# Windowed attention feeding a mixture of experts: searches for the largest w2, scaled w2 operands made in steps, and two row blocks of the last products interleaved

## The chip, the cores and the metric

The kernel runs on one core of a Trainium2 chip. The time is in device microseconds (us), the median of a few executions. The engines are called PE (TensorE, the matmuls), ACT (ScalarE), DVE (VectorE), POOL (GpSimd) and SP (SyncE, which issues all the transfers here).

## The reference

An attention with a window and block summaries, whose output is the input of four experts, mixed with given weights. Cut to what matters:

```python
def _attn_ref(q, k, v):                       # (4, 8, 768, 64), block 32, window 16
    k_sum = k.reshape(B, H, nb, block, D).max(axis=3)
    v_sum = v.reshape(B, H, nb, block, D).mean(axis=3)
    scores_l = where(abs(pos_i - pos_j) < window, scale * q @ k.T, -1e9)
    scores_s = scale * q @ k_sum.T + np.log(block)
    a = softmax(concatenate([scores_l, scores_s], -1))
    return a @ concatenate([v, v_sum], 2)

def _moe_ref(x, domain_probs, w1, w2):        # x 3072 x 512, 4 experts, hidden 1024
    p = domain_probs / (domain_probs.sum(-1, keepdims=True) + 1e-09)
    out = 0
    for e in range(4):
        h = np.maximum(x @ w1[e], 0.0)        # first products
        out += p[:, e:e + 1] * (h @ w2[e])    # second products
    return out
```

All inputs and the output are f32.

## The kernel before, in words

The 3072 tokens are eight blocks of 384 (`TB`). The attention works in 64 pieces; each gives scores (tile `psc` in PSUM), their exponentials (`ms`, with the negated maximum `nb`), a transpose over DRAM (`aw`, `awT`) and the values (`px`), and writes rows of x to DRAM, from where they are read as operands of the experts. f32 numbers are split into a high and a low half, and each product is three matmuls: high by high, high by low, low by high (`hh` and `hl` are the halves of the hidden activations, `xh` and `xl` those of x).

The program is written as a plan of stages (L1191). Three plain stages treat blocks 0 to 1; then the pairs of blocks 1, 2 and 3 follow (`PAIRS`, L807): pair 1 goes through the experts 3, 2, 1, 0, pair 2 through 0, 1, 2, 3, and pair 3 through 3, 2, 1, 0. Each pair and expert is one stage (`pair_units`, L1074). A stage has first products, x by w1, for four groups i of two hidden blocks (f1, f2), in a form with seven products instead of eight (`SEVEN`, L993). Its tiles are `pha` to `phd`: after product 0 ACT copies `pha` into a new `phb`, after product 1 ACT copies `phd` into an SBUF tile `p5`, after product 2 DVE adds it to `phb` to make `phc`, and so on; the later products add onto these. Then the stage has second products, h by w2.

In pairs 1 and 2 the second products are plain (`po` tiles, 128x512). In pair 3, called `SCALED` (L151), they too have the form with seven products (`second_seven`, L1039), in f16 and for three row blocks t of 128 rows in each of the two token blocks. Product m has 12 matmuls of 128x256; the tiles are `poa` to `pod`, named with the expert and t, so that `pob2_1` is tile b of expert 2 and t = 1. After product 0 ACT copies `poa` into `pob`, after product 1 ACT copies `pod` into `p6`; product 2 adds onto `pob`. The copies run under a raised priority (`RUSH`).

To use f16 there, h, w2 and v are scaled by powers of two, which need the largest magnitude of w1 and of w2 for each expert, and of v. `scan` (L751) is called 16 times for an expert, for eight blocks of w1 and eight of w2, each a DVE reduction into a column of `found`. It is called in the stages of pair 1: for w1 in `w1_operands` (L774), for w2 in `pair_units` after products 4 and 5 (L1137). The sixteenth call reduces the columns, and `over_partitions` (L123) takes the maximum over the 128 partitions: 128x2 numbers go to DRAM (`w3d` for expert 3), a second transfer reads them back broadcast to all partitions (`w3e`), DVE reduces that, and `scales` (L131) makes the powers of two. For v the tiles are `vd` and `ve`.

`make_w2` (L811) makes pair 3's scaled w2 operands while pair 2 is computed. There are 16 groups (e, i). One call loads the two raw blocks of a group (`wr2s`, tag `wr` with four buffers), makes four parts and writes each to DRAM (`ws`): a part `wp` is ACT's scaled f16 copy, then DVE's f16 remainder, then a transfer on SP. Between parts POOL makes the differences of the raw blocks in place. Parts 0 and 1 take buffers of tag `wr`, which the raw loads of w1 and w2 use also; parts 2 and 3 take the tag `chunk`, or `ms` once pair 3's x operands exist, with two buffers each. `wp0_23` is part 3 of expert 0's group 2. Calls come after the last first product of group number 1 in pair 2's stages e = 1 to 3 (L1140), and at the unit numbers in `MAKE` (L998) in the second products (`with_fetch`, L946). The stage of pair 3 reads the parts back (`w2s`).

From a point early on (`pinned["rest"] = False`) the order on each engine isn't the written one: a scheduler in the compiler orders the instructions by a timeline of its own, with the written order and the raised priorities as its input. Every engine's instruction goes through one helper line, so all have line 79 in the profile, and the tiles tell them apart.

Of the kernel before, what the change touches and what calls it, by code (L numbers as in the profile page):

```python
# [17 lines left out]
P = 128  # L18
# [48 lines left out]
def attn_moe(ctx: ExitStack, tc: tile.TileContext, qvL, qv0, v0L, kD, kT, vT, w1L, w2L, dpL, cst, out):  # L67
# [54 lines left out]

    def over_partitions(m, k, name):  # L123
        room = dram.tile([P, k], F32, name=f"{name}d")
        SP.dma_start(room, m)
        every = sb.tile([P, P, k], F32, name=f"{name}e", tag="hs", bufs=2)
        flat = room.rearrange("p k -> (p k)").rearrange("(o n) -> o n", o=1)
        SP.dma_start(every.rearrange("p q k -> p (q k)"), flat.broadcast_to([P, P * k]))
        V.tensor_reduce(m, every.rearrange("p q k -> p k q"), axis=AX.X, op=ALU.max)

# [71 lines left out]
    def setup_v(b):  # L202
        vsr = sb.tile([P, G, NB], F32, name=f"vsr{b}", tag="vsr")
        top = facts(G) if b == SCALED else None
        for hp in range(H // 2):
            ch = chunk(f"vch{b}_{hp}")
            load_chunk(b, hp, ch, vT)
            block_stats(ch, vsr, hp, ALU.add)
            if b == SCALED:
                V.tensor_reduce(  # L210
                    top[:, hp : hp + 1], ch, axis=AX.X, op=ALU.max, apply_absolute_value=True
                )
        stack_v(b, vsr)
        if b == SCALED:
            m = facts(1)
            V.tensor_reduce(m, top, axis=AX.X, op=ALU.max)
            over_partitions(m, 1, "v")
            v_scale[b] = scales(m, 1, "v")

# [531 lines left out]
    def scan(e, which, fc, part):  # L751
# [12 lines left out]
        if len(seen) == 2 * FC:  # L764
            m = tops["m"]
            V.tensor_reduce(m, t, axis=AX.X, op=ALU.max)
            over_partitions(m, 2, f"w{e}")
            w_scale[e] = s, inv = scales(m, 2, f"w{e}")
            V.tensor_scalar_mul(s[:, 1:2], s[:, 1:2], W2TOP)
            V.tensor_scalar_mul(inv[:, 1:2], inv[:, 1:2], 1.0 / W2TOP)  # L770

    WS = ("11", "s2", "s1", "s3", "12", "s4", "22")

    def w1_operands(e, pr):  # L774
# [8 lines left out]
        stored[e, pr] = {}  # L783
        scan(e, 0, 2 * pr, r1)
        scan(e, 0, 2 * pr + 1, r2)

# [7 lines left out]
        parts("11", a11, PL)  # L794
        parts("22", a22, V)
        PL.tensor_tensor(a22, a21, a22, op=ALU.add)
        PL.tensor_tensor(a21, a11, a21, op=ALU.subtract)
# [10 lines left out]
    made = {}  # L808
    to_make = [(e, i) for e in PAIRS[-1][1] for i in range(FC // 2)]

    def make_w2():  # L811

        if not to_make:
            return
        e, i = to_make.pop(0)
        s = w_scale[e][0][:, 1:2]
        r1, r2 = (load_weights(w2L, e, 2 * i + j, "2s") for j in range(2))
        r11, r12 = r1[:, 0:256], r1[:, 256:512]
        r21, r22 = r2[:, 0:256], r2[:, 256:512]
        keep = made[e, i] = [dram.tile([P, n, 512], F16, name=f"ws{e}_{i}{n}") for n in (4, 3)]  # L820

        def parts(k, n, raw):
            tag, bufs = ("wr", 4) if k < 2 else ("ms", 2) if SCALED in xpair else ("chunk", CHUNKS)
            t = sb.tile([P, 2, n], F16, name=f"wp{e}_{i}{k}", tag=tag, bufs=bufs)
            A.activation(t[:, 0], raw, AF.Copy, scale=s)
            V.scalar_tensor_tensor(t[:, 1], raw, s, t[:, 0], op0=ALU.mult, op1=ALU.subtract)
            room = keep[k // 2][:, 2 * (k % 2) : 2 * (k % 2) + 2] if k < 3 else keep[1][:, 2]
            SP.dma_start(room if k < 3 else room.rearrange("p (v f) -> p v f", v=2), t)

        parts(3, 256, r11)  # L830
        parts(0, 512, r2)
        PL.tensor_tensor(r11, r12, r11, op=ALU.subtract)
        PL.tensor_tensor(r12, r22, r12, op=ALU.subtract)
        parts(1, 512, r1)
        PL.tensor_tensor(r22, r22, r11, op=ALU.subtract)
        PL.tensor_tensor(r21, r21, r22, op=ALU.subtract)
        parts(2, 512, r2)

# [106 lines left out]

    def with_fetch(units, jobs=()):  # L946
# [92 lines left out]
    def second_seven(pr, e, order, hs, w2):  # L1039
        for t in range(TB // P):  # L1040
            bank = {}

            def new(k):
                room, tag = dict(a=(ps_sc, "sc"), d=(ps_av, "av")).get(k, (ps_mm, "mm"))
                bank[k] = room.tile([P, 512], F32, name=f"po{k}{e}_{t}", tag=tag)[:, 0 : DM // 2]
                return bank[k]

            for m, (k, a, b) in enumerate(SEVEN):
                o = new(k) if m < 2 else bank[k]
                todo = []  # L1050
                for i in order:
                    ah, al = (x[:, t * P : (t + 1) * P] for x in hs[a, i])
                    bh, bl = w2[i][b]
                    todo += [(ah, bh), (ah, bl), (al, bh)]
                for j, (l, r) in enumerate(todo):
                    PE.matmul(
                        o, l, r, start=j == 0 and m < 2, stop=j == len(todo) - 1, skip_group_check=m >= 2
                    )
                with tc.high_priority(offset=RUSH):
                    if m == 0:  # L1060
                        A.copy(new("b"), o)
                    elif m == 1:
                        five = sb.tile([P, TB], F32, name=f"p6{e}_{t}", tag="hs", bufs=2)[:, 0 : DM // 2]
                        A.copy(five, o)
                    elif m == 2:
                        V.tensor_tensor(new("c"), o, five, op=ALU.add)
                    elif m == 4:
                        V.tensor_tensor(bank["d"], o, five, op=ALU.add)
                if m >= 3:
                    k = "adcb"[m - 3]  # L1070
                    add_up((2 * pr + (k in "bd")) * (TB // P) + t, e, bank[k], (k in "cd") * DM // 2)
                yield 2 * len(todo) * US2 / 4, 1.0

    def pair_units(pr, e, last=False):  # L1074
# [11 lines left out]
        for n, i in enumerate(order):  # L1086
# [11 lines left out]
            for m, (k, w, x) in enumerate(SEVEN):  # L1098
# [47 lines left out]
        else:  # L1146
            units = second(tbs, e, hT, w2, last)
        yield from with_fetch(units, MAKE.get((pr, e), ()))

# [132 lines left out]
```

## Time and profile before

| | |
|---|---|
| median of 3 runs | 1194.36 us (1193.41 to 1196.8) |
| the profiled execution | 1199.33 us |
| its span in the trace | 1197.6 us |
| mean granted PE clock | 0.984 |
| PE busy | 1142.4 us, 95% of the span |
| DVE, ACT, POOL busy | 790.8, 634.9, 527.0 us |
| DMA | 275.52 MB, mean 230 GB/s |

By the places of the tiles in the trace, the stages of pair 1 lie at 377 to 446 (e = 3), 446 to 519, 519 to 590 and 590 to 673 us (e = 0); those of pair 2 at 673 to 746 (e = 0), 746 to 815, 815 to 884 and 884 to 953 (e = 3); those of pair 3 at 953 to 1012 (e = 3), 1012 to 1070, 1070 to 1129 and 1129 to 1197 (e = 0).

How to read it: a row of a timeline gives start, duration, engine, line, operation, output tile and input tiles, shapes and types, how many instructions were merged (x), and in brackets the idle time of the engine just before and what ended it. A row of waits gives the tile waited for, its engine or DMA, then total us, times, and the longest.

### The profile page before, as it was taken

How to read it: one execution, taken by the hardware profiler on the slowest of the kernel's cores; microseconds unless marked ns; L12 is line 12 of the kernel's file. 1: busy time of each engine (PE TensorE's matmuls, PEld its weight loads, DVE VectorE, ACT ScalarE, POOL GpSimd, SP SyncE). 2: the span in 40 equal slices, each digit the busy share in tenths (PEclk: the TensorE clock that was granted, in tenths of full speed). 3: DMA queues.
4: the chain of work that ended last, by engine and by line, in shares of the span. 5: the costliest groups of instructions: out<-in, count | busy, mean ns of one | idle time of the engine just before them, and what ended most of it. 6: DMA issues, size and time to landing. Idle time of an engine off the chain costs nothing.

```text
span 1197.6 us, 22374 instructions
## 1 busy us (share of the span) xinstructions
PE 1142.4 (95%) x7620; PEld 1013.5 (85%) x7620; DVE 790.8 (66%) x1834; ACT 634.9 (53%) x1754; POOL 527.0 (44%) x642
## 2 busy tenths in 40 slices
PE   9899899999979999999879899999999999999998
PEld 7788789998968988888778798988888888989896
DVE  6669775657896857668587775765447464646464
ACT  5578667655665636455255564645336261626261
POOL 2398777745876737546246555352115200000000
PEclk9999999999989999999979999999999999999999
DMA  6699797948995888789974799989586771919151
GB/s 235 212 284 303 236 256 229 286 111 249 311 247 147 272 249 231 231 246 305 232 241 111 237 321 287 377 256 344 155 247 223 249 241 29 332 47 323 50 206 54
DMA packets 218753, 275.52 MB, mean 230 GB/s; under 512 B 85136, under 2 KB 123664, under 8 KB 218640
## 3 DMA queue, kind: packets, MB, share of 16 engines
q1 hardware_dynamic: 218640, 274.10, 74.0%
q8 instruction: 60, 0.98, 0.3%
q14 instruction: 53, 0.43, 0.1%
HBM read 185.30 MB, written 71.83 MB: 215 GB/s over the span
## 4 chain that ended last, share of the span: by engine, by line
PE 40%; DMA 4%; DVE 3%; ACT 2%; issue 1%; POOL 1%; SPq 0%; POOLq 0%; ACTq 0%; DVEq 0%
PE po L79 12%; PE phb L79 8%; PE pha L79 5%; PE pob L79 4%; PE phc L79 3%; PE phd L79 2%; PE poa L79 2%; DMA w<-wd 1%; PE poc L79 1%; DMA wr2s<-in_w2L 1%; PE px L79 1%; PE pod L79 1%; PE psc L79 1%; DVE hl L79 1%; POOL wr2s L79 1%
## 5 line engine op out<-in xcount | busy, mean ns | idle before, releaser
L79 PE MATMUL po<-w,hh 128*128 128x512 f32 x1152 | 364.3, 397 | 1.7 <-DVE hl L79 1.7
L79 PEld LDWEIGHTS po<-w,hh 128*128 128x128 f32 x1152 | 213.8, 190 | 47.7 <-DVE hl L79 2.0
L79 PE MATMUL po<-w,hl 128*128 128x512 f32 x576 | 228.1, 398 | 0.0
L79 POOL TENSOR_TENSOR ks<-kr,ks 128x304 fp32r<-128x304 f32 x112 | 99.3, 893 | 124.3 <-ACT ks L79 108.5
L79 ACT ACTIVATE ms<-ms,nb 96x152 f32<-96x152 f32 x256 | 104.3, 415 | 49.9 <-DVE nb L79 49.3
L79 PEld LDWEIGHTS po<-w,hl 128*128 128x128 f32 x576 | 108.8, 189 | 23.8
L79 PE MATMUL phb<-xh_t,w1s 128*128 128x384 f32 x384 | 117.5, 347 | 7.6 <-DVE phc L79 4.4
L79 PE MATMUL pha<-xh,w 128*128 128x384 f32 x384 | 112.2, 338 | 1.9 <-DVE nb L79 1.9
L79 DVE CUSTOM_DVE_ANT_0 ms<-psc,c_sb 96x152 f32<-96x152 f32 x256 | 69.1, 305 | 44.2 <-PE psc L79 41.5
L79 PE MATMUL ph<-xh,wh 128*128 128x384 f32 x256 | 88.1, 348 | 6.0 <-ACT wh L79 4.8
L79 PE MATMUL ph<-xl,wh 128*128 128x384 f32 x256 | 87.5, 342 | 2.4 <-DVE xl L79 2.4
L79 DVE TENSOR_TENSOR aw<-ms,aw 96x512 f16<-96x512 f32 x112 | 77.1, 721 | 18.5 <-ACT aw L79 17.3
L79 ACT CAST aw<-ms 96x512 f16<-96x512 f32 x112 | 53.3, 523 | 66.7 <-issue 42.4
L79 PE MATMUL ph<-xh,wl 128*128 128x384 f32 x256 | 87.3, 342 | 0.3 <-POOL wl L79 0.3
L79 POOL TENSOR_TENSOR wl<-wr,wh 128x512 fp32r<-128x512 f32 x44 | 62.0, 1414 | 44.6 <-ACT wh L79 44.4
L79 PEld LDWEIGHTS phb<-xh_t,w1s 128*128 128x128 f32 x384 | 71.9, 191 | 10.5 <-DVE phc L79 5.2
L79 DVE SCALAR_TENSOR_TENSOR wp<-wr2s,found,wp 128x512 f16<-128x512 f32 (+1 forms) x64 | 50.8, 795 | 45.2 <-ACT wp L79 40.0
L79 ACT CAST ks<-kr 128x304 fp32r<-128x304 f32 x112 | 48.1, 444 | 49.0 <-PE psc L79 31.5
L79 PEld LDWEIGHTS pha<-xh,w 128*128 128x128 f32 x384 | 70.9, 188 | 2.5 <-DVE nb L79 2.2
L79 ACT ACTIVATE wp<-wr2s,found 128x512 f16<-128x512 f32 (+1 forms) x64 | 42.5, 667 | 53.1 <-DMA wr2s<-in_w2L 19.9
L79 PEld LDWEIGHTS psc<-ks,qs 128*96 128x96 f32 x448 | 53.3, 165 | 18.1 <-DVE nb L79 9.8
L79 PE MATMUL psc<-ks,qs 128*96 128x152 f32 x448 | 57.0, 251 | 10.5 <-DVE nb L79 9.5
(209 smaller groups left out, 2794.2 us busy)
## 6 DMA issues: line engine op xcount, KB each, us to landing
w<-wd SPq DMA_DIRECT2D x56, 512.0 KB, 5.5
w1s<-wds SPq DMA_DIRECT2D x112, 256.0 KB, 5.1
w<-wd SPq DMA_DIRECT2D x84, 256.0 KB, 5.1
wr<-in_w1L SPq DMA_DIRECT2D x76, 256.0 KB, 4.3
qv<-in_qvL SPq DMA_DIRECT2D x56, 320.0 KB, 4.4
wd<-w SPq DMA_DIRECT2D x32, 512.0 KB, 4.3
wds<-w1s SPq DMA_DIRECT2D x64, 256.0 KB, 2.8
kr<-in_kD SPq DMA_DIRECT2D x56, 256.0 KB, 4.1
```

Source lines behind the costliest of these rows:

```text
L79: ins = getattr(self.engine, name)(*a, **kw)
```

## The change

Three things are changed.

First, the searches. The calls of `scan` for w2 go from pair 1's first products to its second products, one for each of the units 1 to 8. `over_partitions` becomes two steps: `spread_maxima`, which issues both transfers at unit 10, and `take_maxima`, which reduces and makes the scales at unit 14. v's largest value goes the same way. The calls of `scan` for w1 go behind the first two parts in `w1_operands`.

Second, `make_w2` becomes a generator of 65 steps: the first loads the raw blocks of group 0, and each further step makes one part; the step with a group's first part loads the raws of the next group ahead of it. All four parts take the two buffers of `chunk` or `ms`; none takes `wr`. `MAKE` gives steps in place of groups: every second unit of the second products in pair 2's stages e = 0 to 2 and in pair 3's e = 3 and 2, and every unit in pair 3's e = 1. In pair 2's stages e = 1 and 2 there is a step after each of the four groups of first products.

Third, `second_seven` is written with two row blocks interleaved. Products 0 and 1 of t = 0 and t = 1 come first without the last hidden group, then with it; then products 2 to 6 alternate between the two blocks; t = 2 follows alone.

The diff, cut:

```diff
+    def spread_maxima():
+        for t in pending:
+            m, k, name = t["m"], t["k"], t["name"]
+            room = dram.tile([P, k], F32, name=f"{name}d")
+            SP.dma_start(room, m)
+            t["every"] = every = sb.tile([P, P, k], F32, name=f"{name}e", tag="hs", bufs=2)
...
+            SP.dma_start(every.rearrange("p q k -> p (q k)"), flat.broadcast_to([P, P * k]))
+
+    def take_maxima():
+        while pending and "every" in pending[0]:
+            t = pending.pop(0)
+            V.tensor_reduce(t["m"], t["every"].rearrange("p q k -> p k q"), axis=AX.X, op=ALU.max)
+            t["then"](*scales(t["m"], t["k"], t["name"]))
...
-            over_partitions(m, 2, f"w{e}")
-            w_scale[e] = s, inv = scales(m, 2, f"w{e}")
...
+            pending.append(dict(m=m, k=2, name=f"w{e}", then=then))
...
     def make_w2():
...
+        load(*groups[0])
+        yield
+        for (e, i), after in zip(groups, groups[1:] + [None]):
...
             def parts(k, n, raw):
-            tag, bufs = ("wr", 4) if k < 2 else ("ms", 2) if SCALED in xpair else ("chunk", CHUNKS)
+                tag, bufs = ("ms", 2) if SCALED in xpair else ("chunk", CHUNKS)
...
+            if after:
+                load(*after)
+            parts(3, 256, r11)
+            yield
+            parts(0, 512, r2)
+            PL.tensor_tensor(r11, r12, r11, op=ALU.subtract)
+            PL.tensor_tensor(r12, r22, r12, op=ALU.subtract)
+            yield
...
     def with_fetch(units, jobs=(), e=None, w2=None):
...
+            if w2 and 1 <= n <= FC:
+                scan(e, 1, n - 1, w2[n - 1][0].bitcast(F32))
+            if n == FC + 2:
+                spread_maxima()
+            if n == FC + 6:
+                take_maxima()
             if n in jobs:
-                make_w2()
+                next(making, None)
...
-    MAKE = {(2, 0): (4, 12), (2, 1): (2, 7, 13), (2, 2): (2, 7, 13), (3, 3): (2, 8, 14), (3, 2): (3, 11)}
+    MAKE = {(2, e): range(1, 17, 2) for e in range(3)} | {(3, e): range(1, 21, 2) for e in (3, 2)}
+    MAKE[3, 1] = range(1, 21)
...
     def second_seven(pr, e, order, hs, w2):
-        for t in range(TB // P):
...
+        for js in (range(FC // 2 - 1), range(FC // 2 - 1, FC // 2)):
+            for t in range(2):
+                for m in range(2):
+                    us = product(t, m, js)
+                    if FC // 2 - 1 in js:
+                        after(t, m)
+                    yield us, 1.0
+        for ts, ms in (((0, 1), range(2, len(SEVEN))), ((2,), range(len(SEVEN)))):
+            for m in ms:
+                for t in ts:
+                    us = product(t, m)
+                    after(t, m)
+                    yield us, 1.0
...
-                if m in (4, 5) and pr == PAIRS[0][0]:
-                    fc = (f1, f2)[m - 4]
-                    scan(e, 1, fc, w2[fc][0].bitcast(F32))
-                if m == 6 and n == 1 and pr == SCALED - 1 and e > 0:
-                    make_w2()
+                if m == 6 and pr == SCALED - 1 and e in (1, 2):
+                    next(making, None)
```

What the compiler's scheduler makes of it is seen in the order of the instructions. ACT before, at the start of the second products of pair 3, e = 2; `hh2_3`, `h122_3`, `hs32_3` and `hs42_3` are halves of the last group's hidden activations:

```order
L79 CAST hh2_311_13453<-hr2_3_13437 128x768
L79 COPY pob2_0_13501<-poa2_0_13488 128x256
L79 CAST hh2_3s2_13467<-hr2_3_13437 128x768
L79 CAST h122_3_13481<-hq2_3_13439 128x384
L79 CAST hs32_3_13471<-hk2_3_13438 128x384
L79 COPY p62_0_13516<-pod2_0_13503 128x256
L79 COPY p62_1_13653<-pod2_1_13640 128x256
L79 COPY pob2_1_13638<-poa2_1_13625 128x256
L79 CAST hs42_3_13485<-hq2_3_13439 128x384
```

ACT now, at the same place:

```order
L79 CAST hh2_311_13363<-hr2_3_13347 128x768
L79 COPY pob2_0_13467<-poa2_0_13398 128x256
L79 COPY pob2_1_13481<-poa2_1_13438 128x256
L79 CAST hh2_3s2_13377<-hr2_3_13347 128x768
L79 CAST h122_3_13391<-hq2_3_13349 128x384
L79 CAST hs32_3_13381<-hk2_3_13348 128x384
L79 CAST hs42_3_13395<-hq2_3_13349 128x384
L79 COPY p62_0_13472<-pod2_0_13408 128x256
L79 COPY p62_1_13486<-pod2_1_13448 128x256
```

The copy of block 1's `poa` has moved from behind the two `p6` copies to right behind block 0's. On PE the first two products of blocks 0 and 1 alternate in both orders, up to the first product on `pob`.

ACT before, at the start of pair 3's first stage (e = 3): the first copy `phb3_3_2` of its first group comes right behind the last casts of pair 3's x (`xh3`):

```order
L79 CAST xh3_t2_12067<-xr3_3_12254 128x2x96
L79 CAST xh3_t4_12071<-xr3_3_12254 128x2x96
L79 COPY phb3_3_2_12397<-pha3_3_2_12390 128x384
L79 COPY p53_3_2_12406<-phd3_3_2_12399 128x384
L79 COPY p53_3_3_12489<-phd3_3_3_12482 128x384
L79 COPY phb3_3_3_12480<-pha3_3_3_12473 128x384
```

ACT now, at the same place:

```order
L79 CAST xh3_t4_11993<-xr3_3_12176 128x2x96
L79 ACTIVATE wp0_10_14212<-wr2s0_3_13640,found_74 128x512
L79 ACTIVATE wp0_11_14223<-wr2s0_2_13638,found_74 128x512
L79 ACTIVATE wp0_12_14234<-wr2s0_3_13640,found_74 128x512
L79 ACTIVATE wp0_23_14249<-wr2s0_4_14194,found_74 128x256
L79 ACTIVATE wp0_20_14258<-wr2s0_5_14196,found_74 128x512
L79 ACTIVATE wp0_21_14292<-wr2s0_4_14194,found_74 128x512
L79 COPY phb3_3_2_12319<-pha3_3_2_12312 128x384
L79 COPY p53_3_2_12328<-phd3_3_2_12321 128x384
L79 ACTIVATE wp0_22_14312<-wr2s0_5_14196,found_74 128x512
L79 COPY p53_3_3_12411<-phd3_3_3_12404 128x384
L79 COPY phb3_3_3_12402<-pha3_3_3_12395 128x384
```

Six parts of w2's scaled operands now stand ahead of the first copy, one stands among the copies, and four more follow behind them; before, all 64 parts came ahead of this place. By the order, the first 31 parts now stand between instructions that ran at 658 to 767 us before, none between those at 767 and 885, and 33 from there to those at 970.

SP before, near the end of pair 1's first stage (e = 3), where expert 3's largest values go through DRAM; `w3d` stood 37 rows further up:

```order
L79 DMA wd222_0_5816<-w1222_0_5803 128x512
L79 DMA w3e_5749<-w3d_5747 128x256
L79 DMA wds12_0_5827<-w1s12_0_5799 128x512
L79 DMA wds22_0_5823<-w1s22_0_5798 128x512
L79 DMA wd122_0_5835<-w1122_0_5801 128x512
L79 DMA wds32_0_5831<-w1s32_0_5800 128x512
L79 DMA wr12_4_6289<-in_w1L 128x512
L79 DMA wds42_0_5840<-w1s42_0_5802 128x512
L79 DMA wr12_5_6291<-in_w1L 128x512
```

SP now, at the same place:

```order
L79 DMA wds12_0_5806<-w1s12_0_5778 128x512
L79 DMA wds22_0_5802<-w1s22_0_5777 128x512
L79 DMA wd122_0_5814<-w1122_0_5780 128x512
L79 DMA wds32_0_5810<-w1s32_0_5779 128x512
L79 DMA w3d_6085<-found_74 128x2
L79 DMA wr12_4_6287<-in_w1L 128x512
L79 DMA wds42_0_5819<-w1s42_0_5781 128x512
L79 DMA w3e_6087<-w3d_6085 128x256
L79 DMA wd112_1_6007<-w1112_1_5994 128x512
```

`w3d` and `w3e` are now two transfers apart, at a later place. On DVE the reductions of w2's blocks stand where they stood; the reduction of `w3e` comes later. The places of `vd`, `ve`, `w0d` and `w0e` on SP are unchanged.

More of the change, by code (lines that the diff above doesn't have):

```diff
@@ L216, in setup_v @@
             V.tensor_reduce(m, top, axis=AX.X, op=ALU.max)
-            over_partitions(m, 1, "v")
-            v_scale[b] = scales(m, 1, "v")
+            pending.append(dict(m=m, k=1, name="v", then=lambda *s: v_scale.update({b: s})))
     def stack_v(b, vsr):
@@ L795, in w1_operands @@
         parts("22", a22, V)
+        scan(e, 0, 2 * pr, r1)
+        scan(e, 0, 2 * pr + 1, r2)
         PL.tensor_tensor(a22, a21, a22, op=ALU.add)
@@ L808, in attn_moe @@
     made = {}
-    to_make = [(e, i) for e in PAIRS[-1][1] for i in range(FC // 2)]
     def make_w2():
[L813 to L822, printed above, removed]
-            tag, bufs = ("wr", 4) if k < 2 else ("ms", 2) if SCALED in xpair else ("chunk", CHUNKS)
[L824 to L837, printed above, removed]
@@ new lines, in make_w2, with load, parts @@
+        groups = [(e, i) for e in PAIRS[-1][1] for i in range(FC // 2)]
+        raws = {}
+        def load(e, i):
+            raws[e, i] = [load_weights(w2L, e, 2 * i + j, "2s") for j in range(2)]
+        load(*groups[0])
+        yield
+        for (e, i), after in zip(groups, groups[1:] + [None]):
+            s = w_scale[e][0][:, 1:2]
+            r1, r2 = raws.pop((e, i))
+            r11, r12 = r1[:, 0:256], r1[:, 256:512]
+            r21, r22 = r2[:, 0:256], r2[:, 256:512]
+            keep = [dram.tile([P, n, 512], F16, name=f"ws{e}_{i}{n}") for n in (4, 3)]
+            def parts(k, n, raw):
+                tag, bufs = ("ms", 2) if SCALED in xpair else ("chunk", CHUNKS)
+                t = sb.tile([P, 2, n], F16, name=f"wp{e}_{i}{k}", tag=tag, bufs=bufs)
+                A.activation(t[:, 0], raw, AF.Copy, scale=s)
+                V.scalar_tensor_tensor(t[:, 1], raw, s, t[:, 0], op0=ALU.mult, op1=ALU.subtract)
+                room = keep[k // 2][:, 2 * (k % 2) : 2 * (k % 2) + 2] if k < 3 else keep[1][:, 2]
+                SP.dma_start(room if k < 3 else room.rearrange("p (v f) -> p v f", v=2), t)
+            if after:
[6 more added lines that the diff above has]
+            yield
+            parts(1, 512, r1)
+            PL.tensor_tensor(r22, r22, r11, op=ALU.subtract)
+            PL.tensor_tensor(r21, r21, r22, op=ALU.subtract)
+            yield
+            parts(2, 512, r2)
+            made[e, i] = keep
+            yield
@@ L839, in w2_operands @@
+    making = make_w2()
     def w2_operands(e, i):
@@ L944, in second, with with_fetch @@
             yield from mm2(tb, e, range(TB // P), hT, w2)
-    def with_fetch(units, jobs=()):
+    def with_fetch(units, jobs=(), e=None, w2=None):
         for n, us in enumerate(units):
@@ L1039, in second_seven @@
     def second_seven(pr, e, order, hs, w2):
-        for t in range(TB // P):
[L1041 to L1055, printed above, removed]
+        banks = [{} for t in range(TB // P)]
@@ new lines, in new, with product @@
+        def new(t, k):
+            room, tag = dict(a=(ps_sc, "sc"), d=(ps_av, "av")).get(k, (ps_mm, "mm"))
+            banks[t][k] = room.tile([P, 512], F32, name=f"po{k}{e}_{t}", tag=tag)[:, 0 : DM // 2]
+            return banks[t][k]
+        def product(t, m, js=range(FC // 2)):
+            k, a, b = SEVEN[m]
+            o = new(t, k) if m < 2 and 0 in js else banks[t][k]
+            for j in js:
+                ah, al = (x[:, t * P : (t + 1) * P] for x in hs[a, order[j]])
+                bh, bl = w2[order[j]][b]
+                for v, (l, r) in enumerate(((ah, bh), (ah, bl), (al, bh))):
@@ L1056, in second_seven @@
                     PE.matmul(
-                        o, l, r, start=j == 0 and m < 2, stop=j == len(todo) - 1, skip_group_check=m >= 2
-                    )
[L1059 to L1072, printed above, removed]
+                        o, l, r, start=m < 2 and j == v == 0, stop=j == FC // 2 - 1 and v == 2,
+                        skip_group_check=m >= 2,
+                    )
+            return 3 * len(js) * US2 / 2
+        def after(t, m):
+            bank = banks[t]
+            o = bank[SEVEN[m][0]]
+            with tc.high_priority(offset=RUSH):
+                if m == 0:
+                    A.copy(new(t, "b"), o)
+                elif m == 1:
+                    bank["five"] = sb.tile([P, TB], F32, name=f"p6{e}_{t}", tag="hs", bufs=2)[:, 0 : DM // 2]
+                    A.copy(bank["five"], o)
+                elif m == 2:
+                    V.tensor_tensor(new(t, "c"), o, bank["five"], op=ALU.add)
+                elif m == 4:
+                    V.tensor_tensor(bank["d"], o, bank["five"], op=ALU.add)
+            if m >= 3:
+                k = "adcb"[m - 3]
+                add_up((2 * pr + (k in "bd")) * (TB // P) + t, e, bank[k], (k in "cd") * DM // 2)
@@ L1147, in pair_units @@
             units = second(tbs, e, hT, w2, last)
-        yield from with_fetch(units, MAKE.get((pr, e), ()))
+        yield from with_fetch(units, MAKE.get((pr, e), ()), e, w2 if pr == PAIRS[0][0] else None)
     steps = []
```

17 lines of the change are left out of this document (6 added, 11 removed).

## Prediction

> **What bounds the kernel now.** I read the page first: TensorE is busy for nearly the whole span, so a change pays only where TensorE waits, or runs at a lower clock, in the stages that it touches.
>
> ```profile
> span 1197.6 us, 22374 instructions
> PE 1142.4 (95%) x7620; PEld 1013.5 (85%) x7620; DVE 790.8 (66%) x1834; ACT 634.9 (53%) x1754; POOL 527.0 (44%) x642
> ```
>
> Then TensorE's waits by what ended them (total, times, longest), the rows that concern the last products of pair 3 and the one long wait:
>
> ```profile
> PE psc L79 <- DVE nb L79: 9.5, 1, 9.5
> ...
> PE poa L79 <- ACT hh L79: 3.8, 4, 2.3
> ...
> PE pob L79 <- ACT pob L79: 2.9, 7, 0.5
> ...
> PE poa L79 <- DVE hl L79: 1.5, 4, 0.4
> ...
> PE poa L79 <- DVE acc L79: 0.6, 1, 0.6
> ```
>
> Then the windows of the stages in which w2's scaled operands are made and used: stretch, length, then busy time of PE, PEld, DVE, ACT, POOL, granted clock, DMA share, GB/s. The four stages of pair 2, and pair 3's first:
>
> ```profile
> 673.00:746.00 73.00, 69.62 (x439) 62.02 (x439) 47.96 (x103) 40.84 (x106) 37.62 (x46) 0.98 0.95 298
> 746.00:815.00 69.00, 69.00 (x442) 61.09 (x441) 44.71 (x98) 38.49 (x103) 31.11 (x39) 1.00 0.98 330
> 815.00:884.00 69.00, 67.41 (x405) 59.70 (x405) 30.74 (x79) 26.75 (x77) 13.69 (x18) 1.00 0.76 228
> 884.00:953.00 69.00, 67.13 (x409) 59.09 (x403) 43.16 (x91) 33.28 (x85) 27.06 (x36) 1.00 0.73 235
> 953.00:1012.00 59.00, 55.45 (x387) 50.43 (x386) 32.89 (x59) 25.16 (x50) 0.00 (x0) 0.97 0.47 153
> ```
>
> TensorE lacks 3.38 + 0 + 1.59 + 1.87 = 6.84 us in pair 2: that is all a smoother making of w2 can win there in waits, beside what the clock loses. So the change is worth a few us at most, out of 1199.
>
> **The change part by part.**
>
> *Interleaved row blocks.* The rows around the last products of pair 3, e=2 (TensorE, then ScalarE):
>
> ```profile
> 1049.33 0.61 PE L79 MATMUL poa<-w2s,hh 128*128 128x256 f16 x4 [0.48 <-ACT hh L79]
> 1050.32 0.39 PE L79 MATMUL poa<-w2s,hl 128*128 128x256 f16 x2 [0.39 <-DVE hl L79]
> 1051.05 0.38 PE L79 MATMUL pob<-w2s,hh_0s 128*128 128x256 f16 x2 [0.34 <-ACT pob L79]
> ...
> 1054.43 0.28 PE L79 MATMUL poa<-w2s,h 128*128 128x256 f16 x1
> 1055.25 0.38 PE L79 MATMUL pob<-w2s,hh_0s 128*128 128x256 f16 x2 [0.55 <-ACT pob L79]
> ```
>
> ```profile
> 1050.64 0.36 ACT L79 COPY pob<-poa 128x256 f32<-128x256 f32 x1 [1.37 <-PE poa L79]
> ...
> 1054.81 0.39 ACT L79 COPY pob<-poa 128x256 f32<-128x256 f32 x1
> ```
>
> The order shows that TensorE already ran both blocks' first two products alternately before the change, up to the first pob. So the waits on hh and hl and the first pob wait (3.8, 1.5 and four of the seven in 2.9) stay. What goes is the second: block 1's copy, at 1054.81 behind five other ScalarE steps, now follows block 0's at once, and TensorE's products of block 1 come earlier. The hole from 1054.43 to 1055.25 is 0.82 us where a matmul there takes 0.11 (four in the record of 0.61 at 1049.33, one in the 0.28 at 1054.43: a third of the difference), so 0.71 us. Three stages have it, and the fourth has the acc wait of 0.6 in its place: 4 x 0.7 = **-2.8**. Bounds: 0 if another wait moves in, -3.5 with the restart of the pipeline.
>
> *Raw w2 loaded a group ahead.* The place where the raw load costs TensorE most (its own rows, then ScalarE's and VectorE's):
>
> ```profile
> 677.80 0.44 PE L79 MATMUL phb<-xh_t,w1s 128*128 128x384 f32 x1 [1.49 <-ACT phb L79]
> ...
> 682.08 0.44 PE L79 MATMUL pha<-xh,w 128*128 128x384 f32 x1 [1.89 <-DVE nb L79]
> ```
>
> ```profile
> 679.54 0.72 ACT L79 ACTIVATE wp<-wr2s,found 128x512 f16<-128x512 f32 x1 [1.79 <-DMA wr2s<-in_w2L]
> ```
>
> ```profile
> 680.30 1.26 DVE L79 SCALAR_TENSOR_TENSOR wp<-wr2s,found,wp 128x512 f16<-128x512 f32 x1 [0.25 <-ACT wp L79]
> ```
>
> ```profile
> 680.00:684.00 4.00, 2.11 (x9) 1.93 (x8) 3.27 (x8) 3.26 (x10) 3.55 (x5) 0.82 1.01 276
> 684.00:688.00 4.00, 4.00 (x21) 3.99 (x21) 1.70 (x4) 1.59 (x4) 0.00 (x0) 0.76 1.04 363
> ```
>
> ScalarE stands 1.79 us for the raw weights, VectorE's part follows, the attention's nb comes behind it, and TensorE waits 1.89. Then the granted clock is 0.82 and 0.76 for 4 us each: (0.18 + 0.24) x 4 = 1.7 us more. With the raws a group early that wait is gone: 1.9 + 1.7 = **-3.6**. The 1.49 at 677.80 stays, being a copy behind two parts, not behind a load. The Trainium skill, "TensorE: Matmul & The Clock Gate", section "What's actually happening", has the clock fall after an idle window of about 3.4 us; this trace shows it fall after gaps of 1.89 and 1.49. By that rule the step would give back only its 1.9, and the sum would be 1.7 smaller.
>
> Fewer loads bunched on SP's queue also help the wait on w1s:
>
> ```profile
> 834.17 0.41 PE L79 MATMUL phd<-xh_t,w1s 128*128 128x384 f32 x1 [1.59 <-DMA w1s<-wds]
> ```
>
> In the changed order no part is made between the first 31 and pair 2's last stage, so the queue is freer there, but w1s stays as deep in it; I take half, **-0.8** (bounds 0 and -1.6).
>
> *All parts through two buffers.* A part holds its buffer for ScalarE's half, VectorE's half, the issue and the landing of its write. These are the rows of the 64 parts before (min/median/max; then what they waited for; then landing):
>
> ```profile
> L79 ACT ACTIVATE wp<-wr2s,found x64: 494/722/742, 623.3 to 935.0; 128x512 f16<-128x512 f32 x48, 128x256 f16<-128x256 f32 x16
> L79 DVE SCALAR_TENSOR_TENSOR wp<-wr2s,found,wp x64: 472/752/1378, 624.7 to 936.1; 128x512 f16<-128x512 f32 x48, 128x256 f16<-128x256 f32 x16
> L79 SPq DMA_DIRECT2D ws<-wp x64: 319/322/1215, 625.5 to 936.8; - x64
> ...
>   DMA wr2s<-in_w2L: 19.9, 14
>   POOL wr2s L79: 19.4, 16
> ...
> DMA to landing us min/median/max: 1.7/4.2/7.7
> ```
>
> The engines' waits for raws (19.9) and for GpSimd's differences (19.4) shrink, but the buffer's round trip is 0.72 + 0.75 + 0.32 + 4.2 = 6.0 us, so two buffers give a part each 3.0 us. (At a landing of 1.7 it is 3.5, of 7.7 it is 9.5.) The first 31 parts stand in ScalarE's order against a stretch of 658 to 767, 3.5 us each: it keeps up on the mean, and I take **+1** for uneven places (bounds 0 and +4).
>
> The last 33 stand against 885 to 970, and eleven of them fall past 944, six in a row right ahead of the first phb copy of pair 3:
>
> ```profile
> 953.93 0.46 ACT L79 COPY phb<-pha 128x384 f32<-128x384 f32 x1 [9.20 <-PE pha L79]
> ...
> 969.68 0.52 ACT L79 CAST h<-hq 128x384 f16<-128x384 f32 x1
> ```
>
> ScalarE has 9.20 us free there, from 944.7. Six parts through two buffers take two round trips and two halves: 2 x 6.0 + 1.4 = 13.4, 4.2 us late; at a round trip of 5.5 it is 3.2, at 4.5 it is 1.2, at 3.5 they fit. I take 5.5, a little under the median, as the parts' writes are fewer at a time than before. TensorE has one other product to run in between (six matmuls, 6 x 69.00/442 = 0.9), so 2.3 us of wait and half of the 1.7 of the clock: **+3** (bounds 0 and, at a round trip of 7.0, the end of the eleven: 5 x 7.0 + 0.7 = 35.7 from 944.7 against 970.2, 10.2 late, with the clock +11).
>
> The Trainium skill, "DMA: Bandwidth & Descriptors", section "Anatomy of one DMA", puts the fixed cost of a transfer at about 2.0 us, mostly the receipt of the write. The trace's median of 4.2 disagrees; by 2.0 the round trip would be an estimated 3.8 and the sum 3 us better.
>
> *Searches moved.* The order shows no search of w2 moved on VectorE; only the last reduction, the two transfers and the scales go later. For expert 3 the spread's two transfers now stand together on SP behind the load at 408.39, and VectorE's order has the take behind nb at 414, ahead of a hidden half hl that TensorE's last products need:
>
> ```profile
> w3e<-w3d SPq DMA_DIRECT2D x1, 128.0 KB, 4.3
> ...
> w3d<-found SPq DMA_DIRECT2D x1, 1.0 KB, 7.6
> ```
>
> ```profile
> 408.39 0.63 SPq L79 DMA_DIRECT2D wr<-in_w1L  x1
> ```
>
> ```profile
> 418.39 0.54 DVE L79 SCALAR_TENSOR_TENSOR hl<-phb,hh 128x384 fp32r<-128x384 f32 x1
> ```
>
> ```profile
> 419.97 0.63 PE L79 MATMUL po<-w,hl 128*128 128x512 f32 x2
> ```
>
> At 7.6 + 4.3 us the maxima land at 420.3, hl comes some 5 us late against a slack of 1.0; at a landing of 1.7 for the small one they land at 414.4 and nothing waits. SP too stands at w3e, with two w1 raw loads and copies to DRAM behind it. **+1** (bounds 0 and +4). Experts 2, 1 and 0 have the same form with wider gaps, at nothing; the 9.5 us wait of psc stays, as v's transfers do not move.
>
> *The sum:* -2.8 - 3.6 - 0.8 + 1 + 3 + 1 = **-2.2**; the profiled execution took 1199.33, so 1197.1. That run stands 5.0 above the median of 1194.36; against the median the forecast is **1192.2**.
>
> **The rivals.**
>
> *Slower: two buffers pace ScalarE into pair 3.* Past 944 the DMA engines carry pair 3's weights besides. With a round trip of 7.0 the tail costs +11 in place of +3: -2.2 + 8 = +5.8, 1200.2. For: the parts' median landing is from stretches with no such load; against: the last 19 parts before had short waits. It decides from a landing of about 4.9 (a round trip of 6.7, when the tail passes 9).
>
> *Larger gain: the round trip is short.* At a landing near the least, 1.7, nothing waits in the tail, and all of pair 2's 6.84 goes with its 1.7 of clock: -6.84 - 1.7 - 2.8 + 1 = -10.3, 1184.1. For: the waits for raws and for GpSimd, 39 us in all, have no reason left; against: most of them cost TensorE nothing. The 2.0 us of the Trainium skill's DMA page, named above, would lead here.
>
> *The change does not do what it says.* TensorE's order was interleaved already and the searches stay where they were; if the second pob wait and the raw wait only move on, the time is 1194.4 within 1.
>
> **How the numbers follow.** A measurement of this kernel tells about 0.3% (3.6 us) from no change: 1190.8 to 1198.0 is the same. Forecast 0.50: its terms' bounds, mostly from 1187 to 1197, put 0.22 of it under 1190.8 and 0.28 within. Slower 0.20; larger gain 0.20; nothing 0.10. So faster 0.42, same 0.38, slower 0.20. The range reaches into both outer cases: 1182 to 1201. The forecast's own is 1187 to 1197.
>
> **What would show it.** Right: around 1055 no wait of pob on its copy but one per stage; no wait of ScalarE on wr2s near 680, and clock 1.00 there; ScalarE's parts past 944 starting in pairs 5 to 6 us apart, each pair released by a write's landing; the phb copy at 953.93 some 3 us later against the stage's start; VectorE waiting a few us on w3e. Wrong: landings of the parts' writes under 2 or over 5 us; pair 2's stages shorter by more than 6 us together; a search of w2 at another place in the trace than before; a wait of over 2 us in pair 3's last products.

## The result: slower by one per cent, and the profile after

| | before | after |
|---|---|---|
| median of 5 runs | 1195.94 us (1193.41 to 1198.63) | 1207.08 us (1203.64 to 1209.71) |
| ratio | | 1.0096, 95% interval 1.0068 to 1.0123 |
| the profiled execution | 1199.33 us | 1203.64 us |
| its span | 1197.6 us | 1201.8 us |

The change costs some 11 us. The forecast was 1192.2 us, with a range of 1182 to 1201. The two profiled executions lie only 4.3 us apart, as the one of before (1199.33) is slower than all five runs of before in the table, and the one of after is the fastest of its five; so a stage's length from one execution is worth a few us either way, and totals below rest on the ratios.

The page of after: TensorE is as busy as before, in a longer span.

```profile
span 1201.8 us, 22371 instructions
## 1 busy us (share of the span) xinstructions
PE 1142.3 (95%) x7620; PEld 1012.9 (84%) x7620; DVE 793.0 (66%) x1834; ACT 635.3 (53%) x1754; POOL 522.9 (44%) x642
```

TensorE's waits of after (total, times, longest): the wait of `phb` on ScalarE's copy is 12.8 us, where it was 3.2 before. The pob waits went from 2.9 to 1.2, and one on `poc` is new.

```profile
PE phb L79 <- ACT phb L79: 12.8, 6, 5.7
PE psc L79 <- DVE found L79: 8.8, 1, 8.8
...
PE poa L79 <- ACT hh L79: 3.9, 4, 2.4
...
PE pob L79 <- ACT pob L79: 1.2, 4, 0.3
...
PE pob L79 <- DVE poc L79: 0.8, 3, 0.3
```

The windows of after, for pair 2's four stages and pair 3's first (columns as in the prediction), then pair 3's first stage before, cut at the same places in the program:

```profile
668.20:744.50 76.30, 70.65 (x442) 62.92 (x441) 46.55 (x102) 41.72 (x109) 37.20 (x45) 0.96 0.95 287
744.50:814.70 70.20, 69.03 (x441) 60.97 (x440) 35.75 (x85) 30.08 (x88) 21.77 (x29) 1.00 0.81 263
814.70:883.10 68.40, 68.40 (x439) 60.73 (x438) 31.08 (x79) 26.93 (x79) 13.12 (x17) 1.00 0.71 223
883.10:952.20 69.10, 66.55 (x366) 57.50 (x366) 47.78 (x93) 37.25 (x92) 30.52 (x40) 1.00 0.78 244
952.20:1025.50 73.30, 64.06 (x447) 57.56 (x445) 42.03 (x73) 31.02 (x61) 6.27 (x8) 0.98 0.57 197
```

```profile
952.70:1019.70 67.00, 63.45 (x445) 57.74 (x444) 35.35 (x64) 26.69 (x53) 0.00 (x0) 0.97 0.49 160
```

The loss sits at two places: pair 2's first stage, with 5.65 us without TensorE and a clock of 0.96, and pair 3's first, with 9.24 us (3.55 before).

The 64 parts of w2 in after: ScalarE's and VectorE's own time is what it was, the waits on raw loads (19.9 before) are gone from the list and those on GpSimd's differences fell from 19.4 to 3.9. In their place stand 49.1 us of waiting for the landing of the parts' own writes, 5.1 before.

```profile
L79 ACT ACTIVATE wp<-wr2s,found x64: 492/722/730, 654.1 to 976.0; 128x512 f16<-128x512 f32 x48, 128x256 f16<-128x256 f32 x16
...
  DMA ws<-wp: 49.1, 34
  ACT wp L79: 46.8, 33
  POOL wr2s L79: 3.9, 3
...
DMA to landing us min/median/max: 1.7/3.7/6.2
```

ScalarE in pair 2's first stage: a part at 669.04 filled the second buffer, and the next had to wait 5.37 us for a landing. Behind it, in ScalarE's order, stands the phb copy.

```profile
667.18 0.72 ACT L79 ACTIVATE wp<-wr2s,found 128x512 f16<-128x512 f32 x1 [0.60 <-DMA ws<-wp]
669.04 0.72 ACT L79 ACTIVATE wp<-wr2s,found 128x512 f16<-128x512 f32 x1 [1.14 <-DMA ws<-wp]
669.67 0.94 ACT L79 CAST aw<-ms 96x512 f16<-96x512 f32 x2
675.98 1.12 ACT L79 ACTIVATE wp<-wr2s,found 128x512 f16<-128x512 f32 x2 [5.37 <-DMA ws<-wp]
677.01 0.47 ACT L79 COPY phb<-pha 128x384 f32<-128x384 f32 x1
```

TensorE at the same place, and the windows around it (the granted clock is the third figure from the end):

```profile
677.53 0.69 PE L79 MATMUL phb<-xh_t,w1s 128*128 128x384 f32 x1 [5.65 <-ACT phb L79]
```

```profile
676.00:680.00 4.00, 2.47 (x8) 2.47 (x9) 1.70 (x7) 3.43 (x10) 2.04 (x3) 0.50 1.05 283
680.00:684.00 4.00, 4.00 (x20) 4.00 (x19) 1.13 (x3) 1.60 (x3) 0.18 (x1) 0.79 1.03 383
```

So 5.65 us of idle are followed by a clock of 0.50 and 0.79. The Trainium skill, "TensorE: Matmul & The Clock Gate", section "What's actually happening", puts the fall after about 3.4 us of idle; this gap is longer and agrees, those of 1.49 and 1.89 us in the trace of before do not. The gap of 3.30 us shown next is a little shorter than that and leaves the clock at 1.00 in the windows behind it (960 to 988).

At pair 3's start, ScalarE has the six parts in a row, with 0.53 to 3.57 us of waiting before each (one of the six waits is for GpSimd, the others are for landings), and then the copy that TensorE stood 3.30 us for:

```profile
945.19 0.72 ACT L79 ACTIVATE wp<-wr2s,found 128x512 f16<-128x512 f32 x1 [0.53 <-DMA ws<-wp]
947.59 0.72 ACT L79 ACTIVATE wp<-wr2s,found 128x512 f16<-128x512 f32 x1 [1.68 <-POOL wr2s L79]
949.40 0.72 ACT L79 ACTIVATE wp<-wr2s,found 128x512 f16<-128x512 f32 x1 [1.09 <-DMA ws<-wp]
952.02 0.51 ACT L79 ACTIVATE wp<-wr2s,found 128x256 f16<-128x256 f32 x1 [1.90 <-DMA ws<-wp]
956.10 0.72 ACT L79 ACTIVATE wp<-wr2s,found 128x512 f16<-128x512 f32 x1 [3.57 <-DMA ws<-wp]
958.70 0.72 ACT L79 ACTIVATE wp<-wr2s,found 128x512 f16<-128x512 f32 x1 [1.88 <-DMA ws<-wp]
959.33 0.47 ACT L79 COPY phb<-pha 128x384 f32<-128x384 f32 x1
```

```profile
959.85 0.44 PE L79 MATMUL phb<-xh_t,w1s 128*128 128x384 f32 x1 [3.30 <-ACT phb L79]
```

### The profile page after: what moved, and what is told of

Its sections match the earlier page's. It is cut to its first block, busy times and chain, and to the rows that moved or that the text cites. A ratio compares the mean times of both kernels' runs of the same rounds, so it can differ in the third digit from the quotient of the medians.

```text
span 1201.8 us, 22371 instructions
## 1 busy us (share of the span) xinstructions
PE 1142.3 (95%) x7620; PEld 1012.9 (84%) x7620; DVE 793.0 (66%) x1834; ACT 635.3 (53%) x1754; POOL 522.9 (44%) x642
## 3 DMA queue, kind: packets, MB, share of 16 engines
q1 hardware_dynamic: 218640, 274.10, 73.3%
## 5 line engine op out<-in xcount | busy, mean ns | idle before, releaser
L79 PE MATMUL phb<-xh_t,w1s 128*128 128x384 f32 x384 | 117.9, 348 | 16.9 <-ACT phb L79 12.8
L79 PEld LDWEIGHTS po<-w,hl 128*128 128x128 f32 x576 | 108.6, 189 | 24.3 <-DVE hl L79 0.7
L79 DVE SCALAR_TENSOR_TENSOR wp<-wr2s,found,wp 128x256 f16<-128x256 f32 (+1 forms) x64 | 47.9, 753 | 46.9 <-ACT wp L79 46.8
L79 ACT ACTIVATE wp<-wr2s,found 128x256 f16<-128x256 f32 (+1 forms) x64 | 42.3, 667 | 59.5 <-DMA ws<-wp 49.1
L79 POOL TENSOR_TENSOR qv<-qv,v 128x256 f32<-128x256 f32 x56 | 38.9, 705 | 65.6 <-ACT v L79 64.6
```

Source lines behind the costliest of these rows:

```text
L79: ins = getattr(self.engine, name)(*a, **kw)
```

## The experiments

Twelve kernels were run in four rounds, each against runs of the kernel before in the same round. The theory to test (A) is that the change pays for its two buffers; the rivals are the moved searches (C), the interleaving (B), the place of the parts (D), the steps with raws loaded ahead (E). All ratios in one table, with the lengths of pair 2's four stages together, of pair 3's first stage and of its second, from each kernel's trace. A stage is taken here from where its first products run on their own to where the next stage's do. In pair 3 the next stage's first products already begin among this one's second products (at 1011.42 before, and they run on their own from 1019.73), which is why the first stage has 67.0 us here and 59 in the list of stages ahead of the prediction:

| kernel | ratio (95%) | pair 2, us | pair 3 first, us | second, us |
|---|---|---|---|---|
| before | 1 | 280.0 | 67.0 | 59.5 |
| the change | 1.0096 (1.0068 to 1.0123) | 284.0 | 73.3 | 59.0 |
| only interleaved | 0.9981 (0.9960 to 1.0001) | 279.0 | 65.9 | 59.0 |
| only steps | 1.0125 (1.0092 to 1.0158) | 287.8 | 73.3 | 59.5 |
| only searches | 1.0000 (0.9977 to 1.0023) | 278.4 | 67.0 | 59.5 |
| wr again, raws late | 1.0087 (1.0054 to 1.0121) | 283.4 | 73.4 | 59.0 |
| early slots | 1.0072 (1.0044 to 1.0100) | 284.3 | 65.9 | 58.9 |
| before, two buffers | 1.0063 (1.0040 to 1.0086) | 286.4 | 68.1 | 59.5 |
| constant writes | 1.0208 (1.0178 to 1.0238) | 276.6 | 66.6 | 59.0 |
| no steps | 1.0003 (0.9982 to 1.0024) | 275.7 | 66.6 | 59.0 |
| early slots, four buffers | 0.9999 (0.9981 to 1.0016) | 277.3 | 67.7 | 59.0 |
| early slots, wr, raws late | 1.0039 (1.0019 to 1.0059) | 283.2 | 64.9 | 59.0 |
| before, four buffers | 0.9975 (0.9959 to 0.9991) | 271.8 | 68.6 | 60.8 |
| before, four buffers, interleaved | 0.9929 (0.9903 to 0.9956) | 277.0 | 67.4 | 59.3 |

The four kernels that make w2's parts as before (before, only interleaved, only searches, no steps) spread from 275.7 to 280.0 us in pair 2, so a difference of 4 us between two traces means little there. The four whose parts all go through two buffers and wait for landings (the change, only steps, early slots, before with two buffers) lie at 284.0 to 287.8, clear of that spread.

**One part of the change alone.** The kernel before with one of: the new `second_seven`; the new `make_w2` with `MAKE` and its calls; the new searches.

```diff
     def second_seven(pr, e, order, hs, w2):        # only interleaved
-        for t in range(TB // P):
+        for ts, ms in (((0, 1), range(2, len(SEVEN))), ((2,), range(len(SEVEN)))):
...
-                make_w2()                          # only steps
+                next(making, None)
...
-            over_partitions(m, 2, f"w{e}")         # only searches
+            pending.append(dict(m=m, k=2, name=f"w{e}", then=then))
```

> Only the last products are interleaved. Theory A (the two buffers of w2's parts cost the time, the rest of the change is nearly free): ratio 0.998 to 1.000, each stage of pair 3 after the first 0.3 to 0.5 us shorter than before, the pob wait of 0.55 gone and a wait of pob on poc of 0.27 in its place. Theory B (the interleaving delays ScalarE's or VectorE's steps in pair 3 and costs the 11 us): ratio 1.005 or more, with the first stage of pair 3 longer by several us.

> Only w2's operands are made in steps, with raws a group ahead and all parts in two buffers. Theory A: ratio 1.010 (1.007 to 1.013), ScalarE waits some 45 to 50 us for the landing of its own parts' writes where it was 5.1 before, waits of phb on ScalarE's copies of some 13 us in all on TensorE (3.2 before). Theory B (searches or interleaving cost it): ratio 0.997 to 1.002.

> Only the searches are moved. Theory A: ratio 0.998 to 1.001, pair 1's stages within 1.5 us of before. Theory C (the spread's two transfers, now back to back, stand in SP's queue and hold VectorE): ratio 1.003 or more, VectorE waiting 3 us or more on w3e, w2e or w1e.

Measured: 0.9981, 1.0125 and 1.0000. B and C fall: the whole loss comes with the steps. In the searches' kernel VectorE does wait for `w3e` (2.3 us) and `w1e` (2.2 us), where C expected 3 or more. TensorE has next to no wait in the stage of `w3e` (69.1 of 69.4 us busy). In the stage of `w1e` it waits 1.9 us for `vs` some 13 us later, which the trace of before does not have, and the stage takes 73.8 us (70.6 before), outside the 1.5 us that A allowed; whether the searches cause that was not tried. Pair 1's four stages together take 296.5 us (295.5 before). The interleaving makes each later stage of pair 3 0.5 us shorter, in the trace, and its ratio is not told apart from 1.

**The buffers of wr given back** to the whole change. Since raws ahead and parts can't both have wr's four buffers, the raws are loaded after the last part of the group before.

```diff
-                tag, bufs = ("ms", 2) if SCALED in xpair else ("chunk", CHUNKS)
+                tag, bufs = ("wr", 4) if k < 2 else ("ms", 2) if SCALED in xpair else ("chunk", CHUNKS)
...
-            if after:
-                load(*after)
             parts(3, 256, r11)
...
             made[e, i] = keep
+            if after:
+                load(*after)
```

> The whole change, but parts 0 and 1 take the four buffers of wr again, and a group's raws are loaded after the last part of the group before it, not ahead of the first. Theory A: ScalarE's waits on the parts' writes fall from 49 to under 15 us, waits on raws and on GpSimd come back (10 to 30 us), ratio 0.997 to 1.004. Theory D (it is the place of the parts, ten of which still stand past the last x casts at pair 3's first products, and not the buffers): ratio 1.007 to 1.012 as the whole change, with the 3.3 us wait at pair 3's first phb copy still there.

Measured: 1.0087. Theory A's wait fell as expected, to 6.1 us, and the time did not: D's number came out. But D's wait did not: TensorE no longer waits at the first phb copy (956.93). It waits 2.83 us at the second (962.10), and the clock behind that is 0.62 (964 to 968). ScalarE's parts past 944 now wait for raws, and that holds the copies:

```profile
950.45 0.51 ACT L79 ACTIVATE wp<-wr2s,found 128x256 f16<-128x256 f32 x1 [3.71 <-DMA wr2s<-in_w2L]
...
956.93 0.47 ACT L79 COPY phb<-pha 128x384 f32<-128x384 f32 x1
...
960.96 0.51 ACT L79 ACTIVATE wp<-wr2s,found 128x256 f16<-128x256 f32 x1 [3.55 <-DMA wr2s<-in_w2L]
...
962.10 0.49 ACT L79 COPY phb<-pha 128x384 f32<-128x384 f32 x1
```

So one wait was exchanged for another, and place and buffers had to be parted by other kernels.

**Other slots, same buffers.** All parts come ahead of pair 3's x casts; the first 31 keep their place.

```diff
-    MAKE = {(2, e): range(1, 17, 2) for e in range(3)} | {(3, e): range(1, 21, 2) for e in (3, 2)}
-    MAKE[3, 1] = range(1, 21)
+    MAKE = {(2, e): range(1, 17) for e in range(4)}
```

> The whole change with another table of slots: every step comes in pair 2's second products, and by the order all 64 parts stand ahead of pair 3's last x casts; the first 31 stand as in the whole change, the two buffers stay. Theory D (what costs most is the parts among pair 3's first products): pair 3's first stage back from 73 to 66 or 68 us, ratio 1.001 to 1.005, what is left coming from pair 2. Theory A (the two buffers cost wherever the parts stand): the wait of ScalarE on the parts' writes stays at 40 us or more, and the stages of pair 2 lose what pair 3 wins: ratio 1.007 to 1.012.

Measured: 1.0072. Pair 3's first stage is back at 65.9 us, as D has it; the wait on the writes stays (47.7 us) and pair 2 stays at 284.3 (284.0 in the change). The ratio is in A's range, but pair 2 does not lose what pair 3 wins, as A had it: the trace shows 7.4 us won in pair 3, the ratios only some 3, and their intervals overlap.

**Two buffers in the kernel before,** and nothing else.

```diff
-            tag, bufs = ("wr", 4) if k < 2 else ("ms", 2) if SCALED in xpair else ("chunk", CHUNKS)
+            tag, bufs = ("ms", 2) if SCALED in xpair else ("chunk", CHUNKS)
```

> The kernel before, with parts 0 and 1 also taken from the two buffers of chunk or ms: groups, raw loads and the table of slots stay; by the order no part stands past pair 3's last x casts. Theory A: ScalarE waits 30 us or more on the parts' writes, pair 2's first stage takes 75 to 77 us as in the whole change (73.5 before), ratio 1.002 to 1.006. Theory D: ratio 0.999 to 1.002, since nothing is moved into pair 3.

Measured: 1.0063, a little above A's range; 0.6% from one line. The ScalarE wait of A, and pair 2's first stage:

```profile
ACT wp L79 <- DMA ws<-wp: 47.2, 27, 6.4
```

```profile
667.40:744.10 76.70, 71.50 (x441) 63.53 (x440) 46.23 (x105) 41.39 (x109) 37.28 (x45) 0.96 0.93 285
```

No wait on raws is left in this kernel's list either, though nothing is loaded ahead: the parts no longer take the raw loads' buffers. So what the loading ahead was to give comes already with the tag. The tag also changes what the scheduler does: with no part in wr, the first part is made at 653 us and not at 623. That later start is not the cost, since the four-buffer kernels below have it too (653 and 660).

**No wait for a landing:** in the whole change the transfers write constants, and a buffer is free when VectorE is done.

```diff
-                SP.dma_start(room if k < 3 else room.rearrange("p (v f) -> p v f", v=2), t)
+                same = c_sb[:, :n].bitcast(F16).rearrange("p (v f) -> p v f", v=2)
+                SP.dma_start(room if k < 3 else room.rearrange("p (v f) -> p v f", v=2), same)
```

> The whole change, but the transfers of the parts write constants instead of the parts, so a part's buffer comes free with VectorE's half and nothing waits for a landing; the scaled w2 operands hold constants, and SP issues these transfers earlier. Five parts still stand past pair 3's last x casts. If waits on landings are the cause: pair 2's first stage 70 to 73 us and pair 3's first 65 to 68 us, ratio 0.995 to 1.001. If it is ScalarE's and VectorE's own time for the parts, some 0.7 us each: pair 3's first stage 70 us or more, ratio 1.004 or more.

Measured: 1.0208, which neither side expected. The constants depend on nothing, so all 64 of their writes were issued from 16.5 to 64.9 us. A load of w1 that SP issued at 44.5 us before came behind them, at 65.9, and TensorE stood 24.3 us for it, from 48 to 72:

```profile
PE ph L79 <- ACT wh L79: 24.3, 1, 24.3
```

Past that, pair 2's first stage takes 73.6 us and pair 3's first 66.6, near and within what the first theory gave. But with the waits the writes themselves have left these stages (DMA share 0.85 in pair 2's first, 0.95 in the change), so this run does not tell whether the waits or the traffic cost the time, and as a time it decides nothing.

**Searches and interleaving, without the steps.**

> The searches moved and the last products interleaved, w2's parts made as before. By the single parts (0.9981 and 1.0000): ratio 0.996 to 1.000, no wait of ScalarE on the parts' writes over 10 us in all, pair 3's first stage 66 us. If the parts of the change act on each other: ratio over 1.002.

Measured: 1.0003, just above the first range. ScalarE waits 6.6 us on the parts' writes and pair 3's first stage takes 66.6, as expected. The rest of the change is worth nothing that can be measured, in sum.

**Four buffers.** In the first two kernels the parts alternate between `chunk` and `ms`: once in the whole change with the early slots, once in the kernel before. The third has the early slots with `wr` and late raws.

```diff
-                tag, bufs = ("ms", 2) if SCALED in xpair else ("chunk", CHUNKS)
+                tag, bufs = ("ms", 2) if k % 2 else ("chunk", CHUNKS)
```

> The early table of slots with the whole change, but the parts alternate between chunk and ms, which makes four buffers, two of which the attention's exponentials share; steps and raws ahead stay. Theory A (two buffers cost 8 to 9 us wherever the parts stand): ScalarE's wait on the parts' writes falls from 48 to 10 to 25 us, pair 2's four stages together 276 to 281 us (284 with two buffers), ratio 0.997 to 1.003. Theory E (steps and raws ahead crowd the queue, the buffers are only where that shows): pair 2 stays at 283 us or more, ratio 1.005 to 1.009.

> The kernel before with its parts alternating between chunk and ms, four buffers, none in wr. Theory A: ratio 0.998 to 1.002 where two buffers gave 1.0063, ScalarE's wait on the parts' writes 10 to 25 us (47 with two). If the buffers taken from wr matter by the raws and not by their number: ratio 1.004 or more.

> The early table with parts 0 and 1 in the four buffers of wr and a group's raws loaded after the last part of the group before it. Theory A: pair 3's first stage 66 to 67 us, pair 2 276 to 281 us, ratio 0.997 to 1.002. Theory E: the waits on raws take the place of the waits on the writes, pair 2 at 283 us or more, ratio 1.004 to 1.008.

Measured: 0.9999, 0.9975 (a little below A's range) and 1.0039. With steps and raws ahead kept, going from two buffers to four takes 1.0072 to 0.9999; in the kernel before, 1.0063 to 0.9975. E falls with these. In the third, A missed: it lands just under E's lower end, with pair 2 at 283.2 us and 24.0 us of waiting on raws, so parts in wr and raws that come late hold ScalarE as well. ScalarE's waits of the kernel before with four buffers, and its window of pair 2's first stage, in which TensorE has no hole and the full clock:

```profile
ACT wp L79 <- POOL wr2s L79: 14.0, 8, 3.3
ACT wp L79 <- DMA ws<-wp: 11.6, 10, 2.4
ACT wp L79 <- DMA wr2s<-in_w2L: 2.6, 3, 1.4
```

```profile
666.90:734.90 68.00, 68.00 (x441) 60.99 (x440) 36.23 (x88) 33.27 (x95) 24.73 (x32) 1.00 0.83 253
```

In this kernel sixteen parts stand past pair 3's x casts, more than the change's eleven. They run from 974 to 1049, later than the change's, and none of them waits for a landing of its own writes, though some wait up to 3.3 us for GpSimd. Pair 3's first stage takes 68.6 us and its second 60.8, some 3 us more than before in all, where the change has 73.3 and 59.0.

**Both gains together:** four buffers and the interleaving on the kernel before.

> The kernel before with four buffers for the parts (chunk and ms in turn, none in wr) and with the last products interleaved; searches, groups, raw loads and slots stay. If the two gains measured apart (0.9975 and 0.9981) add: ratio 0.994 to 0.997, pair 3's last three stages 59 us each, pair 2 at 272 us. If the sixteen parts that stand in pair 3 take the interleaving's gain: ratio 0.997 to 0.999.

Measured: 0.9929 (0.9903 to 0.9956), below both ranges; the upper end of the interval is the product of the two, 0.9956; median 1186.82 us against 1193.4. Pair 3's later stages came out as expected (59.3, 59.0 and 58.3 us), pair 2 at 277.0 and not 272, which is within the spread of one trace. It is faster than before, which the change is not. Why by more than the two parts make was not tried.

## Why the prediction was wrong

- **All parts through two buffers** is the step that failed. It took +1 for pair 2, since "it keeps up on the mean" (3.0 us a part against 3.5). The round trip was sized well: 0.72 + 0.75 + 0.32 + 3.7 = 5.5 us from after's rows, 6.0 forecast. But the parts come close together, often two at once (675.98), the landing there has a median of 5.1 us (664 to 716), and ScalarE held the phb copy at 677.01 behind the part that waited, so TensorE stood 5.65 us. The mean rate says nothing about that. In place of +1 the traces show +4.0 in pair 2 (284.0 against 280.0; 284.0 to 287.8 against 275.7 to 280.0 for the two groups of kernels above). The change of one line to two buffers costs 1.0063 by itself, 7.5 us, and by its trace most of that in pair 2 (286.4).
- **Raw w2 loaded a group ahead,** -3.6, was not won. The wait on raws at 680 did go; the wait for a landing took its place a few us earlier, longer (5.37 against 1.79 us), and with a lower clock behind it (0.50 and 0.79 against 0.82 and 0.76). What was late next was the buffer, and the step did not ask.
- **The eleven parts past 944** were taken at +3 and measured 73.3 - 67.0 = +6.3 in that stage of one execution. Mechanism and place were right: the parts are released by landings, one by one and not in pairs, and the copy at 953.93 came 5.9 us later by the stage's start (959.33 - 952.20 = 7.1 against 953.93 - 952.70 = 1.2). The size was not. The landing there has a median of 4.9 us (944 to 980), a round trip of 6.7, at which the prediction let its slower rival begin, while the step took 5.5; and the clock, for which it had added 0.85, stayed at 1.00. The slower rival named this mechanism at 1200.2 with a chance of 0.20, and put its whole price into these parts; pair 2's share was left out, which is why even the range missed.
- **The wait on w1s at 834,** -0.8: gone in after, whose stage there takes 68.4 us (70.2 before). But it takes 68.4 and 68.6 with only the searches or only the interleaving as well, so the raw loads are not shown to be the reason.
- **Interleaving,** -2.8: right in kind, and in size as far as the traces tell. With only the interleaving, three stages of pair 3 are 0.5 us shorter each, not 0.7, and the first one is 1.1 us shorter; the ratio, 0.9981, is 2.3 us and not told apart from nothing. The 0.55 wait went, and 0.27 on `poc` is new, which is the next thing late in the sevenfold form. The rows of pair 3, e = 2, after:

```profile
1056.81 0.38 PE L79 MATMUL pob<-w2s,hh_0s 128*128 128x256 f16 x2 [0.34 <-ACT pob L79]
...
1063.14 0.60 PE L79 MATMUL pob<-w2s,hs 128*128 128x256 f16 x4 [0.27 <-DVE poc L79]
```

- **Searches moved,** +1: the wait came where it was put. The maxima were there at 413.6, near the 414.4 of the lower bound, and the slack took it. Expert 1, taken at nothing, has a wait of 2.55 us on VectorE too. The ratio shows nothing (1.0000).

```profile
413.56 0.42 DVE L79 TENSOR_REDUCE found<-w3e 128x2 f32<-128x256 f32 x1 [2.56 <-DMA w3e<-w3d]
```

- **The larger gain** needed a round trip of 3.5 us, and the landings were longer. The Trainium skill, "DMA: Bandwidth & Descriptors", section "Anatomy of one DMA", led there with its fixed cost of about 2.0 us; landings of a median of 3.7 us in after, and 5.1 in the crowded stretch, disagree. The Trainium skill has this cost there for transfers that GpSimd issues, and without the time of the bytes; the writes here are issued by SP and carry 128 or 256 KB, so the two are not the same thing.

What stays open: how the 11 us divide between buffers and place. The change and its early slots (1.0096 and 1.0072) have overlapping intervals; only steps against before with two buffers (1.0125 and 1.0063) do not, which speaks for the parts among pair 3's first products adding to it (steps and raws ahead cost nothing by the four buffers). In the kernel with sixteen parts later in pair 3, none of which waits for a landing, they add some 3 us in the trace.

## What to carry to other kernels

A staging buffer that a transfer must release belongs in the sum with the transfer's landing in the crowded stretch, and against the bursts in which its engine uses it, not against the mean rate: two buffers cost 7.5 us here where the mean fitted, and four cost nothing measurable. When a change takes a buffer pool from one use to cure a wait, price the pool that takes over first; on ScalarE, which here worked in order, one part's wait was also the wait of the copies behind it. Run the one-line edit alone before the rewrite: here the tag was most of the loss, and the same line with four buffers was a small gain (0.9975).

## What was not expected of the hardware

The landing of the parts' writes in after has a median of 5.1 us from 664 to 716, at a DMA share of 0.95, of 3.0 us from 883 to 944, at 0.76, and of 4.9 us from 944 to 980, at 0.98, where pair 3's weights are loaded too:

```profile
DMA to landing us min/median/max: 2.0/5.1/6.1
```

```profile
DMA to landing us min/median/max: 1.7/3.0/4.7
```

```profile
DMA to landing us min/median/max: 2.6/4.9/5.5
```

And transfers that depend on nothing are not free: in the constant-writes kernel the first 40 us have a DMA share of 0.99 (0.59 before), with no loss to TensorE yet. The loss came from 48 to 72 us, when the load of w1 that stood behind the writes on SP was late; of the 40 us from 40 to 80, TensorE was busy for 15.7 (34.9 before).

```profile
0.00:40.00 40.00, 38.61 (x298) 31.01 (x299) 25.24 (x112) 23.72 (x65) 8.61 (x25) 1.00 0.99 361
```

```profile
0.00:40.00 40.00, 38.35 (x296) 30.74 (x297) 25.02 (x112) 23.53 (x65) 8.59 (x25) 1.00 0.59 204
```
